# One chunk of RWKV-7 attention plus SwiGLU: the decayed neighbours of `a` laid out by distance first, and one ScalarE copy per level for both kept halves of K

## The chip, the cores and the metric

The kernel runs on one core of a Trainium2 chip. The metric is the device time of one execution in microseconds; the median of three runs is quoted. A core has five engines that each work through their own list in order: TensorE (PE, with weight loads shown as PEld), VectorE (DVE), ScalarE (ACT), GpSimd (POOL) and SyncE (SP). They wait for one another through semaphores. Transfers go through queues that SP, POOL and, at the start, ACT issue into.

## The reference

Two blocks, one after the other. The first is RWKV-7 attention over 4 batches, 8 heads, 768 steps and head size 40 (32 sequences in all), the second a SwiGLU feed-forward over the 3072 tokens of width 320 with hidden size 1536.

```python
for t in range(S):
    y[:, :, t] = np.einsum('bhd,bhde->bhe', rt, state)
    Sa = np.einsum('bhde,bhe->bhd', state, at)
    state_decay = state * wt[:, :, None, :] - np.einsum('bhd,bhe->bhde', Sa, bt)
    state = state_decay + np.einsum('bhd,bhe->bhde', vt, kt)
...
rms = np.sqrt(np.mean(x * x, axis=-1, keepdims=True) + 1e-06)
xn = x / rms * rms_g
g = xn @ w_gate
out = (g * (1.0 / (1.0 + np.exp(-g))) * (xn @ w_val)) @ w_out
```

## The kernel before, in words

**Chunks.** The 768 steps are cut into 24 chunks of C = 32. Inside a chunk the recurrence becomes a triangular system: how strongly step s reaches a later step t is the product of a vector of s (k or b), a vector of t (a), and all decays w between them. `front(c)` (line 654) loads a chunk, turns it on TensorE so that the 40 channels lie on partitions, and builds the triangular matrix LT and the decayed keys KN. `inverse(c)` (or `early_inverse` for the first four chunks) inverts the triangle on VectorE in small steps, with trips to DRAM and back. `main(c)` makes the outputs and the next state. `feed(g)` runs the feed-forward for every second chunk. `front` runs two chunks ahead of `main`.

**Levels.** LT is filled by five levels l = 1, 2, 4, 8, 16: at level l a segment of 2l steps is split in halves, and entries cross from the left half to the right one. K holds the keys of both kinds, k and b (the code's `x in range(2)`, the two "crossings"), 32 steps each; A holds `a`. After each level the left halves of K are multiplied by the decay of the right half, and the right halves are kept as they are; A likewise for the other side.

**Levels 1 and 2 in one step.** Inside a group of four steps there are six pairs: three at distance 1, two at distance 2, one at distance 3. The tile A holds, for each of 16 sequences on a partition block (NI) and each of 8 groups (g), seven vectors, some of them `a` itself and some `a` times decays. ScalarE copies three of them out of PSUM (line 681). VectorE makes entries 3 and 4 from entries 1 and 2 and the decays (line 690), and entry 6 from entry 4 (line 691). One set of small matmuls ("gramk", lines 693 and 694) multiplies K with all 56 columns of A into PSUM. Then three masked copies on VectorE (the helper `where`, a `copy_predicated`, lines 696 to 699) pick entries for distances 1, 2 and 3 out of PSUM into LT under the mask `near`. Lines 708 to 710 build from A the next level's tile Ab. The distances' first columns stand at 0, 3 and 6 of a group's seven.

**Levels 4, 8 and 16** (lines 713 to 750) each run gramk from Ab, one masked copy into LT under `msk`, a ScalarE copy of KN out of PSUM, a product of K's left halves on VectorE, and the copy of K's right halves into the other K tile on ScalarE (lines 730 and 731), once for each of the two crossings.

**Order.** Every operation is recorded as a piece; pieces wait for those that wrote or read the same elements. Nothing is scheduled at run time: the string ORDER lists, by place among the pieces not yet issued, which piece comes next, and a dash puts in a matmul that only keeps TensorE running (line 1017). PAIRS says which of three PSUM pairs each PSUM tile ("room") uses. Each engine's list follows from that order. Helpers record most operations, so profile lines are those of helpers: L446 is every VectorE operation, L469 a ScalarE copy, L488 a matmul, L491 a transpose.

Of the kernel before, what the change touches and what calls it, by code (L numbers as in the profile page):

```python
# [9 lines left out]
U32 = mybir.dt.uint32  # L10
# [7 lines left out]
P = 128  # L18
# [15 lines left out]
85 84 76 83 58 78 73 86 74 59 60 75 5 89 61 88 53 77 80 4 43 6 201 7 87 90 44 8 334 62 9 - - - - - - - - 93 10 18 79  # L34
11 12 214 557 13 213 567 14 15 94 566 210 16 17 95 558 108 200 - - - 97 96 19 335 20 21 2 209 22 23 98 25 199 568 26
100 578 202 24 101 107 569 111 57 - - - - - 102 106 124 589 27 122 112 392 109 103 52 119 113 104 54 577 155 125 110
204 105 120 - - - - - - 114 203 117 121 559 211 598 118 46 131 129 132 45 562 560 212 597 563 588 561 394 123 115 136
586 384 133 134 - - - - - 126 130 116 47 564 3 145 383 135 336 128 137 48 144 143 141 587 219 142 51 570 127 565 146
138 337 55 573 1005 216 579 281 393 220 582 608 571 390 234 379 239 607 572 583 580 380 251 574 222 38 221 609 575 581
42 - - - - - - - - 223 82 226 339 91 64 227 338 39 81 139 224 263 576 238 153 56 249 247 590 206 584 228 382 237 591  # L40
272 593 40 233 232 585 381 154 148 594 33 140 205 229 592 389 235 250 28 248 - - 325 236 32 245 36 230 147 260 282 391
246 259 150 35 34 326 595 0 36 270 155 214 148 242 243 62 605 598 230 - 239 40 616 599 601 628 64 49 91 600 602 30 48
626 1135 28 257 603 29 241 68 150 255 65 0 1347 194 0 194 84 173 0 - - - 182 540 200 0 557 184 1 186 935 542 540 0 506
515 527 257 513 300 0 111 97 110 61 112 96 51 439 458 122 50 243 480 0 244 0 58 255 242 0 259 709 104 120 246 708 247
456 470 258 488 719 0 256 470 457 242 0 716 265 487 104 0 268 0 0 265 473 0 262 277 0 273 0 236 0 260 0 269 0 461 241
- - - - - - - 237 242 0 0 278 242 243 252 0 252 0 0 89 0 99 246 0 97 0 230 94 440 0 230 94 440 231 - - - - - - - - -
240 441 244 0 0 468 440 451 255 0 42 468 269 469 258 215 440 239 204 0 0 257 253 203 93 449 92 212 0 235 - - - - - - -
- 246 0 437 0 262 0 246 247 436 245 464 470 258 259 469 260 244 - - 255 471 465 468 466 0 215 466 269 256 445 697 255
478 686 93 94 264 95 687 270 96 266 97 0 97 470 695 2 98 99 3 100 471 101 473 1 102 0 468 99 470 100 471 101 441 102
103 258 104 105 260 106 - - - - - - - - - - - 0 504 106 107 473 108 0 108 502 0 108 109 469 110 111 0 0 0 0 0 - - 13 0  # L50
374 16 146 143 14 147 142 15 13 355 - - - 25 386 358 0 358 386 388 16 387 389 25 390 79 17 391 28 70 147 355 191 69
356 80 148 149 26 359 0 28 2 29 149 0 149 150 29 0 149 31 185 391 23 32 390 29 150 356 151 186 33 389 0 151 29 387 152
27 40 187 153 154 155 156 33 157 158 159 160 161 34 162 36 163 164 37 165 41 391 38 42 392 39 394 561 166 395 393 552
0 42 548 395 209 0 560 165 42 395 548 210 43 428 211 427 557 44 - - - 565 166 558 45 167 549 168 0 566 168 739 565 567
738 571 169 579 - - 45 728 572 0 124 139 0 535 682 0 535 545 140 578 536 141 0 547 545 546 543 578 0 558 554 567 0 519
- - - - - - 517 377 696 378 380 381 695 518 120 685 135 526 - - - - - - 522 686 379 527 382 136 530 383 554 529 121 -
- 141 540 123 523 565 539 122 537 142 125 538 124 524 - - - - 145 525 148 534 149 152 154 551 535 147 555 - - 157 146
# [3 lines left out]
607 367 478 34 568 - - 35 830 594 36 567 820 38 - 476 37 571 366 570 0 605 356 433 434 435 436 120 437 0 317 318 319  # L61
320 441 321 322 323 324 355 456 458 459 442 4 357 325 457 326 327 328 443 0 443 328 329 330 331 357 0 35 331 3 0 37
450 359 3 36 358 331 332 357 333 356 0 462 448 330 461 464 331 332 468 364 447 463 31 467 476 458 333 365 334 335 0
425 439 441 302 426 436 0 6 439 2 0 435 332 2 436 443 444 0 448 332 442 334 443 333 340 449 0 297 329 342 32 330 - 3
33 341 334 0 332 331 0 332 293 441 295 333 0 438 0 436 333 336 295 337 309 438 338 1 375 342 310 365 374 515 27 292 0
362 292 26 28 44 339 29 34 27 32 338 0 646 29 34 336 647 32 0 439 64 315 647 339 440 634 441 63 340 0 287 413 606 312
313 607 623 12 314 615 414 0 410 310 411 603 619 27 412 475 413 620 414 415 621 416 311 633 28 417 812 418 312 625 - -
- - 476 313 419 420 421 822 258 314 422 423 0 810 423 625 637 477 2 0 819 2 257 0 420 421 645 310 422 0 - - - - - 310
422 3 313 32 630 311 423 33 643 424 641 631 312 0 0 637 20 635 420 647 613 21 421 611 648 819 23 38 22 422 809 423 39
659 24 3 612 36 818 424 651 25 808 621 425 59 660 426 249 427 58 0 427 3 25 428 249 4 28 47 0 - 614 428 429 28 430 431  # L70
0 26 25 614 617 484 31 27 627 0 458 590 400 600 401 0 12 582 32 401 33 583 25 0 579 30 21 - - - - - - - - - 588 29 591
22 453 397 428 398 605 23 0 23 429 24 609 0 590 24 397 588 602 1 604 398 601 429 430 399 2 427 0 584 - - - - - - - - -
- - - - - 4 397 0 25 397 4 0 393 394 28 21 23 27 395 598 24 22 424 607 0 35 395 37 396 24 2 424 47 397 398 38 399 400
# [4 lines left out]
976 716 416 663 729 634 977 562 563 717 713 986 665 564 565 566 975 567 401 568 714 569 985 570 571 967 572 723 722 -  # L78
0 403 726 402 572 401 573 0 726 738 736 573 739 574 664 575 737 576 577 3 723 751 578 579 760 580 747 581 582 633 583
4 584 0 584 585 634 586 636 587 635 588 734 633 0 746 588 - - - - - 403 757 589 722 590 3 404 591 592 593 594 595 596  # L80
# [290 lines left out]
def kernel(  # L371
# [42 lines left out]
    NI = 2 * N  # L414
# [239 lines left out]
    def front(c):  # L654
# [19 lines left out]
        o = 0  # L674
# [375 lines left out]
```

## Time and profile before

| what | us |
|---|---|
| three runs | 1083.66, 1079.48, 1078.9 |
| median | 1079.48 |
| span of the profiled execution | 1078.2 |
| TensorE busy | 1010.2 |
| VectorE busy | 834.2 |
| ScalarE busy | 462.2 |
| GpSimd busy | 309.0 |

The profiled execution is a run of its own, and its own time is known from its span alone: first to last instruction, without what lies before and after. A busy engine is one that has an instruction in work; on TensorE matmuls overlap, so being busy is not being at its peak. The stretch views give the busy time of each engine in a piece of the span. The group rows give how often an instruction with a shape ran, its total and its mean in ns, and then the idle time ahead of it with what ended that.

### The profile page before, as it was taken

To read this page: it belongs to the slowest core of one execution; us is meant where nothing else is said; L and a number is where in the kernel's file an instruction comes from. 1 tells how busy PE (TensorE), PEld (TensorE's weight loads), DVE (VectorE), ACT (ScalarE), POOL (GpSimd) and SP (SyncE) were. 2 spreads that over 40 slices of the span, in tenths; PEclk is the share of its full clock that TensorE was granted. 3 is DMA by queue.
4 is the path that set the end of the run, shared out by engine and by line. 5 is a ranking of instruction groups with operands and counts; after the bars stand their busy time and mean duration, and the time that the engine had idled before them with its cause. 6 is when DMAs were issued, how large, how long until landed. Compare 5 with 4: busy or idle time off the path is not lost. (4 is left out here: it accounts for less than half of the span.)

```text
span 1078.2 us, 53465 instructions
## 1 busy us (share of the span) xinstructions
PE 1010.2 (94%) x23406; PEld 828.3 (77%) x23406; DVE 834.2 (77%) x2861; ACT 462.2 (43%) x1043; POOL 309.0 (29%) x554
## 2 busy tenths in 40 slices
PE   6767899999999999999999999998999999999998
PEld 6766778777888787877788778887777887887776
DVE  7887879876868888887897888887788889797420
ACT  6845756643543433532443434433344344342211
POOL 9714404120532223241331331331332331200000
PEclk9778999999999999999999999999999999999999
DMA  9965448766564364574465654665545553744242
GB/s 180 196 155 123 73 106 220 213 127 177 124 142 122 99 150 116 144 145 120 96 152 133 146 126 112 142 142 123 126 106 110 134 150 90 162 109 123 77 140 86
DMA packets 172456, 143.34 MB, mean 133 GB/s; under 512 B 125504, under 2 KB 143872, under 8 KB 172224
## 3 DMA queue, kind: packets, MB, share of 16 engines
q1 hardware_dynamic: 153856, 116.96, 42.4%
q0 software_dynamic: 16192, 22.64, 12.2%
q8 instruction: 184, 3.01, 1.2%
q10 hardware_dynamic: 2176, 0.33, 0.2%
q14 instruction: 48, 0.39, 0.1%
HBM read 123.86 MB, written 15.99 MB: 130 GB/s over the span
## 5 line engine op out<-in xcount | busy, mean ns | idle before, releaser
L488 PE MATMUL ps<-xg,wf 128*128 128x256 f32 (+1 forms) x1728 | 355.2, 392 | 4.7 <-DVE xg L446 1.1
L488 PEld LDWEIGHTS ps<-xg,wf 128*128 128x128 f32 (+1 forms) x1728 | 261.6, 189 | 60.4 <-issue 16.9
L488 PE MATMUL po<-wf,hT 128*128 128x320 f32 x576 | 180.1, 445 | 0.1
L446 DVE TENSOR_TENSOR tmp<-Yi,M 128x60 f32<-128x60 f32 (+24 forms) x620 | 129.5, 209 | 19.7 <-DMA M<-sB 6.9
L446 DVE TENSOR_TENSOR Yi<-Yi,tmp 128x60 f32<-128x60 f32 (+24 forms) x620 | 130.2, 210 | 12.7 <-DVE ss L446 0.2
L466 ACT ACTIVATE sg<-ps 128x256 f32<-128x256 f32 x144 | 52.4, 383 | 192.4 <-PE ps L488 182.7
L488 PEld LDWEIGHTS po<-wf,hT 128*128 128x128 f32 x576 | 102.6, 191 | 34.0 <-issue 1.7
L485 POOL DMA_DIRECT2D VU<-in_v_dram x92 | 53.6, 587 | 234.2 <-PE ps L488 157.0
L446 DVE TENSOR_TENSOR hT<-ps,sg 128x256 f32<-128x256 f32 x144 | 59.0, 419 | 62.4 <-ACT sg L466 55.9
L469 ACT COPY KN<-ps 128x640 f32<-128x640 f32 x96 | 66.2, 691 | 76.6 <-PE ps L491 27.9
L488 PEld LDWEIGHTS ps<-Ab,K 40*64 40x64 f32 x4608 | 78.3, 139 | 26.4 <-issue 8.5
L446 DVE TENSOR_TENSOR K<-K,T 128x512 f32<-128x512 f32 (+1 forms) x192 | 93.3, 495 | 4.2 <-ACT K L469 2.1
L488 PE MATMUL ps<-Ab,K 40*64 40x56 f32 x4608 | 88.0, 225 | 8.8 <-ACT K L469 3.7
L485 POOL DMA_DIRECT2D kbn<-in_b_dram x92 | 53.4, 584 | 147.9 <-PE ps L488 147.0
L446 DVE TENSOR_TENSOR As<-ps,msi 128x256 f32<-128x256 f32 (+1 forms) x186 | 79.2, 475 | 18.3 <-PE ps L488 17.4
L469 ACT COPY K<-K 128x256 f32<-128x256 f32 (+1 forms) x168 | 71.8, 443 | 41.3 <-PE ps L488 20.3
L488 PEld LDWEIGHTS ps<-As,KN 128*40 128x40 f32 x3072 | 64.6, 122 | 15.1 <-issue 9.7
L485 POOL DMA_DIRECT2D wn<-in_w_dram x92 | 51.6, 565 | 83.7 <-DVE KN L446 34.7
L485 POOL DMA_DIRECT2D kbn<-in_k_dram x92 | 53.5, 585 | 73.8 <-PE ps L488 73.5
L488 PE MATMUL ps<-As,KN 128*40 128x32 f32 x3072 | 71.1, 203 | 3.7 <-issue 2.7
L446 DVE TENSOR_TENSOR y<-y,ps 128x256 f32<-128x256 f32 x119 | 49.9, 419 | 19.7 <-PE ps L488 17.6
L446 DVE COPY_PREDICATED LT<-near,ps 128x384 f32<-128x384 uint32 (+2 forms) x72 | 52.3, 727 | 3.6 <-PE ps L488 1.9
(133 smaller groups left out, 1544.5 us busy)
## 6 DMA issues: line engine op xcount, KB each, us to landing
wf<-sW SPq DMA_DIRECT2D x144, 480.0 KB, 4.3
M<-sB SPq DMA_DIRECT2D x80, 128.0 KB, 3.8
rn<-in_r_dram SPq DMA_DIRECT2D x24, 160.0 KB, 4.5
sW<-ex SPq DMA_DIRECT2D x16, 240.0 KB, 4.3
out_dram<-o SPq DMA_DIRECT2D x48, 80.0 KB, 3.9
kbn<-in_k_dram POOLq DMA_DIRECT2D x92, 40.0 KB, 3.5
kbn<-in_b_dram POOLq DMA_DIRECT2D x92, 40.0 KB, 3.3
wan<-in_a_dram POOLq DMA_DIRECT2D x46, 80.0 KB, 4.7
```

The costliest lines, as they stand in the source:

```text
L446: plan.add("DVE", kind, lambda at: fn(at(o), *m(at)), [o], aps(*args))
L466: plan.add("ACT", "act", lambda at: nc.scalar.activation(at(o), at(a), f, **kw), [o] + aps(acc), [a])
L469: plan.add("ACT", "copy", lambda at: nc.scalar.copy(at(o), at(a)), [o], [a])
L485: plan.add(by, "dma", lambda at: queue.dma_start(out=o, in_=i), [o], [i])
L488: return o, lhsT, rhs, lambda at: nc.tensor.matmul(at(o), lhsT, rhs, start=start, stop=stop, skip_group_check=True)
```

## The change

A is laid out as NI x 7 x 8 in place of NI x 8 x 7: for a sequence the eight groups of one entry now lie side by side, where before the seven entries of one group did. All that touch A follow: the copy out of PSUM, the products, gramk's right operand (still 56 floats in a row), the PSUM result (g4) and the masked copies, which now go entry by entry and within an entry over the eight groups. LT, `near`, the decays T and the tile Ab keep their layout; they are walked in the new order. Apart from that the two copies of K's right halves at levels 4, 8 and 16 become one over both crossings. ORDER names the pieces of the same order with the dropped copies left out, so its numbers differ; in each pair the single copy stands either where the first or where the second stood.

```diff
-    A_ = Turns(1, [P, NI, 8, 7], "A", whole)
+    A_ = Turns(1, [P, NI, 7, 8], "A", whole)
...
-        copy(A[:, :, :, 0:3], a4.rearrange("p n (g j) -> p n g j", j=4)[:, :, :, 1:4])
+        copy(A[:, :, 0:3], a4.rearrange("p n (g j) -> p n j g", j=4)[:, :, 1:4])
...
-        w4 = Tl[1].rearrange("p n (g j) -> p n g j", j=4)
         t2 = Tl[2].rearrange("p n (g x) -> p n g x", x=2)
-        tt(A[:, :, :, 3:5], A[:, :, :, 1:3], w4[:, :, :, 1:3], MUL)
-        tt(A[:, :, :, 6], A[:, :, :, 4], w4[:, :, :, 1], MUL)
+        w_j = Tl[1].rearrange("p n (g j) -> p n j g", j=4)
+        tt(A[:, :, 3:5], A[:, :, 1:3], w_j[:, :, 1:3], MUL)
+        tt(A[:, :, 6], A[:, :, 4], w_j[:, :, 1], MUL)
         gr = plan.room().rearrange("p o (n t) -> p o n t", n=N)
         pe("gramk", [mm(gr[half(i), o, n, 0:56], K[part(o), 2 * n + i].rearrange("p x s -> p (x s)"),
-                        A[part(o), 2 * n + i].rearrange("p g j -> p (g j)")) for n, i, o in each])
-        g4 = gr.rearrange("p o n t -> p (o n) t")[:, :, 0:56].rearrange("p n (g j) -> p n g j", j=7)
+                        A[part(o), 2 * n + i].rearrange("p j g -> p (j g)")) for n, i, o in each])
+        g4 = gr.rearrange("p o n t -> p (o n) t")[:, :, 0:56].rearrange("p n (j g) -> p n j g", g=8)
         for dist, at in ((1, 0), (2, 3), (3, 6)):
             m = 4 - dist
-            where(LT.rearrange("p n (g j) -> p n g j", j=4)[:, :, :, dist:], near[:, dist - 1:dist].rearrange(
-                "p u (g j) -> p u g j", j=4)[:, :, :, dist:].bitcast(U32).to_broadcast((P, NI, 8, m)), g4[:, :, :, at:at + m])
+            where(LT.rearrange("p n (g j) -> p n j g", j=4)[:, :, dist:], near[:, dist - 1:dist].rearrange(
+                "p u (g j) -> p u j g", j=4)[:, :, dist:].bitcast(U32).to_broadcast((P, NI, m, 8)), g4[:, :, at:at + m])
...
         for x in range(2):
-            tt(Ab[:, :, 16 * x:16 * x + 16].rearrange("p n (h j) -> p n h j", j=4)[:, :, :, 1:4], A[:, :, x::2, 0::3],
-               w4[:, :, x::2, 0:1].to_broadcast((P, NI, 4, 3)), MUL)
+            tt(Ab[:, :, 16 * x:16 * x + 16].rearrange("p n (h j) -> p n j h", j=4)[:, :, 1:4], A[:, :, 0::3, x::2],
+               w_j[:, :, 0:1, x::2].to_broadcast((P, NI, 3, 4)), MUL)
...
-            for x in range(2):
-                copy(side(K1[:, :, x], l, 1), side(K[:, :, x], l, 1))
+            both = lambda t_: side(t_.rearrange("p n x s -> p (n x) s"), l, 1)
+            copy(both(K1), both(K))
```

More of the change, by code (lines that the diff above doesn't have):

```diff
@@ L39 @@
[L39 to L53, printed above, removed]
@@ L62 @@
[L62 to L66, printed above, removed]
@@ L72 @@
-22 453 397 428 398 605 23 0 23 429 24 609 0 590 24 397 588 602 1 604 398 601 429 430 399 2 427 0 584 - - - - - - - - -
-- - - - - 4 397 0 25 397 4 0 393 394 28 21 23 27 395 598 24 22 424 607 0 35 395 37 396 24 2 424 47 397 398 38 399 400
[4 rows of a table removed]
-976 716 416 663 729 634 977 562 563 717 713 986 665 564 565 566 975 567 401 568 714 569 985 570 571 967 572 723 722 -
-0 403 726 402 572 401 573 0 726 738 736 573 739 574 664 575 737 576 577 3 723 751 578 579 760 580 747 581 582 633 583
-4 584 0 584 585 634 586 636 587 635 588 734 633 0 746 588 - - - - - 403 757 589 722 590 3 404 591 592 593 594 595 596
[147 rows of a table removed]
+85 84 76 83 58 78 73 86 74 59 60 75 5 89 61 88 53 77 80 4 43 6 198 7 87 90 44 8 328 62 9 - - - - - - - - 93 10 18 79
@@ new lines @@
+11 12 211 548 13 210 558 14 15 94 557 207 16 17 95 549 108 197 - - - 97 96 19 329 20 21 2 206 22 23 98 25 196 559 26
+100 569 199 24 101 107 560 111 57 - - - - - 102 106 123 580 27 121 112 386 109 103 52 113 104 54 568 152 124 110 119
+201 105 - - - - - - 114 200 117 120 550 208 589 118 46 130 128 45 553 551 209 588 554 579 552 388 122 115 134 577 378
+131 132 - - - - - 125 129 116 47 555 3 142 377 133 330 127 135 48 141 139 578 216 140 51 561 126 556 143 136 331 55
+564 993 213 570 275 387 217 573 599 562 384 231 373 236 598 563 574 571 374 247 565 219 38 218 600 566 572 42 - - - -
@@ new lines @@
+- - - - 220 82 223 333 91 64 224 332 39 81 137 221 258 567 235 150 56 245 243 581 203 575 225 376 234 582 266 584 40
+230 229 576 375 151 145 585 33 138 202 226 583 383 232 246 28 244 - - 319 233 32 242 36 227 144 255 276 385 254 147 35
+34 320 586 0 36 264 152 211 145 239 240 62 596 589 227 - 236 40 607 590 592 619 64 49 91 591 593 30 48 617 1120 28 594
+29 238 68 147 251 65 0 1329 189 0 189 81 170 0 - - - 178 531 194 0 548 180 1 182 923 533 531 0 497 506 518 251 504 294
+0 109 96 108 61 95 51 433 452 119 50 240 474 0 241 0 58 252 239 0 256 703 102 117 243 702 244 450 464 255 482 713 0
@@ new lines @@
+253 464 451 239 0 710 261 481 102 0 264 0 0 261 467 0 258 272 0 268 0 233 0 256 0 264 0 455 238 - - - - - - - 234 239
+0 0 272 239 240 249 0 0 0 87 0 96 243 0 94 0 227 91 434 0 227 91 434 228 - - - - - - - - - 237 435 241 0 0 462 434 445
+251 0 42 462 263 463 253 212 434 236 201 0 0 252 200 90 443 89 209 0 232 - - - - - - - - 242 0 431 0 256 0 242 243 430
+241 458 464 253 254 463 240 - - 250 465 459 462 460 0 212 460 263 251 439 691 250 472 680 90 91 258 92 681 264 93 260
+94 0 94 464 689 2 95 96 3 97 465 98 467 1 99 0 462 96 464 97 465 98 435 99 100 252 101 102 254 103 - - - - - - - - - -
@@ new lines @@
+- 0 498 103 104 467 105 0 105 496 0 105 106 463 107 108 0 0 0 0 0 - - 13 0 371 16 143 140 14 144 139 15 13 352 - - -
[3 rows of a table added]
+43 425 208 424 554 44 - - - 562 163 555 45 164 546 165 0 563 165 733 562 564 732 568 166 576 - - 45 722 569 0 121 136
+0 532 676 0 532 541 137 572 533 138 0 543 541 542 539 572 0 553 549 561 0 516 - - - - - - 514 374 690 375 377 378 689
+515 117 679 132 523 - - - - - - 519 680 376 524 379 133 527 380 549 526 118 - - 138 120 520 559 536 119 534 139 122
+535 121 521 - - - - 142 522 145 531 146 149 151 547 532 144 550 - - 154 143 546 533 147 152 148 551 162 558 150 157
@@ new lines @@
+685 161 158 686 0 158 683 159 162 1 0 542 670 0 503 41 551 42 553 43 419 504 986 552 44 987 45 560 506 420 430 434 433
+421 431 568 505 438 432 441 46 569 823 439 0 569 439 582 832 570 574 0 832 45 442 574 46 822 584 570 586 443 572 47
+594 48 597 11 840 585 571 440 608 593 830 0 11 440 370 595 0 580 590 601 367 475 34 565 - - 35 824 589 36 564 814 38 -
[3 rows of a table added]
+329 436 331 437 330 337 443 0 294 326 339 32 327 - 3 33 338 331 0 329 328 0 329 290 435 292 330 0 432 0 430 330 333
+292 334 306 432 335 1 372 339 307 362 371 509 27 289 0 359 289 26 28 44 336 29 34 27 32 335 0 640 29 34 333 641 32 0
@@ new lines @@
+433 64 312 641 336 434 628 435 63 337 0 284 407 600 309 310 601 617 12 311 609 408 0 404 307 405 597 613 27 406 469
+407 614 408 409 615 410 308 627 28 411 803 412 309 619 - - - - 470 310 413 414 415 813 255 311 416 417 0 801 417 619
+631 471 2 0 810 2 254 0 414 415 638 307 416 0 - - - - - 307 416 3 310 32 624 308 417 33 636 418 634 625 309 0 0 630 20
+628 414 639 607 21 415 605 640 810 23 38 22 416 800 417 39 650 24 3 606 36 809 418 643 25 799 615 419 59 651 420 246
+421 58 0 421 3 25 422 246 4 28 47 0 - 608 422 423 28 424 425 0 26 25 608 611 478 31 27 0 452 584 593 394 395 0 12 576
@@ L228 @@
+32 395 33 577 25 0 573 30 21 - - - - - - - - - 582 29 585 22 447 391 422 392 23 0 23 423 24 601 0 584 596 24 391 582
+595 1 392 594 423 424 393 2 421 0 578 - - - - - - - - - - - - - - 4 391 0 25 391 4 0 387 388 28 21 23 27 389 590 24 22
[5 rows of a table added]
+395 559 705 560 973 561 562 955 563 714 713 - 0 397 717 396 563 395 564 0 717 728 726 564 729 565 655 566 727 567 568
+3 714 740 569 570 748 571 736 572 573 624 574 4 575 0 575 576 625 577 627 578 626 579 724 624 0 735 579 - - - - - 397
[145 rows of a table added]
 """
```

15 lines of the change are left out of this document (removed), and 310 rows, old and new, of the table ORDER.

## The prediction

> **What bounds the kernel now.** I read the page first, for each engine's load; then stretches of 45 us, for where TensorE stands still; then the groups with shapes kept apart, for prices; last the chain of waits and the timeline, for what reaches the end.
>
> ```profile
> PE 1010.2 (94%) x23406; PEld 828.3 (77%) x23406; DVE 834.2 (77%) x2861; ACT 462.2 (43%) x1043; POOL 309.0 (29%) x554
> ```
> ```profile
> 0.00:45.00 45.00, 32.56 (x656) 29.71 (x657) 37.67 (x101) 33.23 (x67) 41.68 (x93) 0.90 0.95 176
> 45.00:90.00 45.00, 32.98 (x832) 29.88 (x831) 32.49 (x114) 26.32 (x50) 10.92 (x22) 0.76 0.68 164
> 450.00:495.00 45.00, 44.21 (x973) 35.89 (x972) 40.34 (x152) 18.66 (x44) 11.70 (x20) 1.00 0.63 142
> 855.00:900.00 45.00, 42.97 (x972) 35.15 (x971) 37.77 (x138) 18.30 (x44) 14.68 (x25) 1.00 0.52 123
> ```
>
> In the stretches the columns after the length are PE, PEld, DVE, ACT and POOL busy. TensorE is nearly full in the middle (44.2 and 43.0 of 45 us) and loses 12 us in each of the first two stretches, so little can be won later on. VectorE is second with 5 to 7 us of idle time in each middle stretch, ScalarE has half of its time free. What makes an engine other than TensorE faster can win only where TensorE waits for it; what makes VectorE slower costs whatever its idle time does not take up. Here is what it does around the instructions that change, from the chain of waits:
>
> ```profile
> 905.44 0.66 DVE LT L446
> 906.12 0.74 DVE LT L446
> 907.30 0.64 DVE LT L446
> ...
> 937.14 0.73 DVE LT L446
> 937.89 0.74 DVE LT L446
> 938.65 0.72 DVE LT L446
> 939.44 0.81 PE ps L488 x64
> ```
>
> These are the three masked copies into LT (the `where` loop, lines 696 to 699) of two late chunks. All six are links of the chain that ended last; after the second triple TensorE starts at once.
>
> **The change, part by part.** Orders first: on TensorE, VectorE, GpSimd and SyncE the program has the same instructions in the same order; ScalarE has 72 fewer. No transfer, queue or semaphore partner is added, and the moving operand of the matmuls stays 56 floats in a row. So the time goes by the durations of the instructions with new access patterns.
>
> ```profile
> L446 DVE COPY_PREDICATED LT<-near,ps 128x128 f32<-128x128 uint32 x24 | 17.5, 729 | 0.4
> L446 DVE COPY_PREDICATED LT<-near,ps 128x256 f32<-128x256 uint32 x24 | 17.4, 726 | 0.3
> L446 DVE COPY_PREDICATED LT<-near,ps 128x384 f32<-128x384 uint32 x24 | 17.4, 726 | 2.9 <-PE ps L488 1.9 <-DMA out_dram<-o 0.8
> L446 DVE COPY_PREDICATED LT<-msk,ps 128x256 f32<-128x256 uint32 x72 | 31.2, 433 | 13.8 <-PE ps L488 8.8 <-ACT KN L469 3.8
> L446 DVE TENSOR_TENSOR T<-T 128x128 f32<-128x128 f32 x24 | 6.8, 285 | 0.1
> L446 DVE TENSOR_TENSOR T<-T 128x256 f32<-128x256 f32 x24 | 10.1, 420 | 4.0 <-ACT T L469 3.9
> ```
>
> *Masked copies.* The striking thing is that 128, 256 and 384 elements take the same 726 to 729 ns, while the later levels' masked copies do 256 in 433. In the first three, 128 groups (16 sequences by 8) are walked, with 3, 2 or 1 elements each: the price is per group. The two T rows give an ordinary slope of (420 - 285) / 128 = 1.05 ns an element; then 433 - 256 x 1.05 = 164 ns is a masked copy's fixed part, and a group costs (729 - 164) / 128 = 4.4 ns, however many of its four neighbours are taken. Why per group? Three operands step there: LT and `near` by 4 floats from group to group, PSUM by 7. The cost is the same for one element as for three, though three cover more of PSUM; what all three share is one 4-float place in LT and one in `near` per group. I put the price there.
>
> After the change the inner loop runs over the 8 groups for one distance, then over the next. That is exactly the walk that the 729 ns instruction does already (LT and `near` by 4 floats, one element at each stop; only PSUM goes from steps of 7 to steps of 1). So 384 elements become three such walks: 164 + 3 x 565 = 1859 ns, 256 two: 1294, 128 one: 729. Sum 3.88 us instead of 2.18: **+1.70 us a chunk**. The other end: if the PSUM step alone is the price, it goes, and at 1.05 ns an element they take 567, 433 and 298 ns, -0.88 us. I take +1.70, since the 729 ns row is the nearest there is.
>
> [...]
>
> *The products.*
>
> ```profile
> L446 DVE TENSOR_TENSOR A<-A,T 128x256 f32<-128x256 f32 x24 | 11.0, 460 | 3.5 <-ACT T L469 3.5
> L446 DVE TENSOR_TENSOR A<-A,T 128x128 f32<-128x128 f32 x24 | 9.6, 398 | 0.2
> L446 DVE TENSOR_TENSOR Ab<-A,T 128x192 f32<-128x192 f32 x48 | 20.9, 441 | 0.2
> ```
>
> The second walks lone elements (A by 7, w by 4) and takes 398 against 285 for 128 closer elements: with a fixed part of 285 - 128 x 1.05 = 150 ns that is 1.94 ns an element. Afterwards A lies in a row but w (in T) is still read by 4 or 8, and Ab is written by 4. Bounds: 420 to 150 + 256 x 1.94 = 647 for the first, 285 to 398 for the second, 352 to 522 for each of two Ab. Against 460 + 398 + 2 x 441 that is -0.35 to +0.35 us a chunk; I take +0.35, as a lone step remains in each. VectorE in all: +2.05 us a chunk, 49 us over 24.
>
> *ScalarE.*
>
> ```profile
> L469 ACT COPY K<-K 128x256 f32<-128x256 f32 x144 | 55.7, 405 | 40.9 <-PE ps L488 20.3 <-DVE K L446 14.5 <-issue 4.8
> L469 ACT COPY K<-K 128x512 f32<-128x512 f32 x24 | 16.2, 673 | 0.4
> L469 ACT COPY A<-ps 128x384 f32<-128x384 f32 x24 | 13.9, 581 | 3.4 <-PE ps L491 3.4
> L469 ACT COPY Ab<-ps 128x128 f32<-128x128 f32 x24 | 9.6, 398 | 4.2 <-PE ps L491 4.2
> L469 ACT COPY M<-ps 128x128 f32<-128x128 f32 x8 | 2.2, 272 | 5.5 <-PE ps L488 4.3 <-DMA wf<-in_moe_w_out_dram 1.2
> L469 ACT COPY T<-ps 128x512 f32<-128x512 f32 x24 | 14.2, 591 | 15.2 <-PE ps L491 10.9 <-DVE tmp L446 2.9 <-DVE Yi L446 1.3
> L469 ACT COPY K<-ps 128x1024 f32<-128x1024 f32 x24 | 24.3, 1011 | 19.0 <-PE ps L491 19.0
> ```
> ```profile
> PEld ps L488 <- ACT K L469: 11.0, 12, 3.8
> PE ps L488 <- ACT K L469: 7.2, 5, 3.7
> ```
> ```profile
> 739.64 0.71 ACT L469 COPY K<-K 128x256 f32<-128x256 f32 x2
> ```
>
> Two copies of 256 become one of 512: 2 x 405 to at most 673 (that row steps by 2; this one has runs of 4, 8 or 16). Neighbouring copies overlap, a pair is through in 0.71 us (last row), so a pair wins some 0.04 to 0.1 us. The single copy must wait for both crossings' halves of K, where the first of two waited for one; behind it stands most often the KN copy, for whose PSUM room a later gram waits. In the program's order 28 of the 72 pairs stand together; of the other 44 the single copy stands at the first one's place in 18, at the second's in 25, in between once. At the first's place it is ready sooner and delays what stood between (mostly KN copies) by 0.27 us; at the second's it ends up to 0.27 us later. TensorE waits for these copies 18.2 us in 17 waits. 17 x 0.27 = 4.6 us either way is the bound; I take 0.
>
> A's copy out of PSUM now reads by 4 floats. Bounds: from 591 - 128 x 0.83 = 484 ns (slope (1011 - 591) / 512) up to that plus 384 x (398 - 272) / 128 = 862. I take +0.28 us, by the Ab row, and cost it at nothing: ScalarE next stands 19.0 us in all, 0.8 a chunk, waiting for TensorE before K's copy. Without that cover it costs 24 x 0.28 = 6.7 us.
>
> *What reaches the end.* VectorE is in order, so all behind the masked copies moves: the K products, the next level's masked copy, the inverse's steps, hT. Who waits: the gram matmuls of the next level, hence KN and K on ScalarE. In the two chunks of the chain all 2.05 us count. For the two before them I read the slack from the timeline, between the last masked copy and the gram matmuls that follow:
>
> ```profile
> 823.61 0.73 DVE L446 COPY_PREDICATED LT<-near,ps 128x128 f32<-128x128 uint32 x1
> ...
> 860.48 0.72 DVE L446 COPY_PREDICATED LT<-near,ps 128x128 f32<-128x128 uint32 x1
> ```
> ```profile
> 825.48 1.16 PE L488 MATMUL ps<-Ab,K 40*64 40x56 f32 x64
> ...
> 862.03 1.16 PE L488 MATMUL ps<-Ab,K 40*64 40x56 f32 x64
> ```
>
> That is 825.48 - 824.34 = 1.14 and 862.03 - 861.20 = 0.83 us, which leaves 0.91 and 1.22 late. The mean of four is 1.56 us a chunk, 37 us for 24. TensorE's idle 1 to 2 us of each 45 us takes up part of a lateness from chunk to chunk; I estimate a fifth, which leaves **+30 us**. The span is 1078.2 us, 1.3 below the median of 1079.5 (runs 1078.9 to 1083.7); I add to the median: 1109.5, say **1109 us**. Ends of this case: half of the 24 delays count in full and the others not at all, less the product term, 12 x 1.35 = +16 (1095), to all 49 us (1128).
>
> **Rivals.**
>
> *PSUM's step of 7 was the price* (the faster side). Place: the same three copies. It decides if the 729 ns fall to about 298 when only the PSUM step changes. For it: PSUM is what differs most from the 433 ns row (there 16 floats in a row). Against: equal time for one, two and three PSUM elements. Price: -0.88 + 0.35 = -0.53 us a chunk, down to -1.2 with the low products; where the copies are on the chain (2 of 4) that is 12 x 0.53 = -6 to 12 x 1.2 = -15: 1065 to 1073, say 1072. [...]
>
> *A lone stop costs a masked copy what it costs a product*, 1.94 ns an element, and the rest was PSUM. Then 164 + 1.94 x (384, 256, 128) = 909, 661, 412, sum 1.98: -0.20, with the products +0.15 us. By 1.56 / 2.05 of that, 24 x 0.11 = +3 us: 1082. For it: the 398 ns row has the same steps in SBUF. Against: it needs PSUM to make up just the difference in all three.
>
> **How the numbers follow.** Forecast 0.72, PSUM rival 0.17, middle rival 0.11. About 0.5% (5.4 us) is what a measurement of this kernel can tell from no change, so same is 1074 to 1085. The forecast falls whole on slower, the PSUM rival on faster (0.16, with 0.01 too small to tell), the middle one mostly on same (0.09; 0.02 slower with ScalarE's +4.6). Faster 0.16, same 0.10, slower 0.74. The range 1077 to 1127 takes the forecast and the middle rival and leaves out the PSUM rival and the top.
>
> **What would show it.** Masked copies of 1.86, 1.29 and 0.73 us: the forecast's price. 0.57, 0.43, 0.30: the PSUM rival. 0.91, 0.66, 0.41: the middle. The 128-element copy alone decides, since only its PSUM step changes. Products near 640, 400 and 520 ns; A's copy near 860; K copies near 620 to 670 and 72. VectorE near 883 us busy; TensorE's busy time about as now, so its idle time up by the 30 us. Wrong I would be if VectorE gets the 49 us and TensorE's idle time does not grow: then its slack is larger than in the four chunks read.

## The result and the profile after

The changed kernel takes **1121.35 us** (median of 6 runs, 1111.99 to 1128.05) where the kernel before takes 1079.19 us (6 runs): a ratio of 1.0361, 95% interval 1.0313 to 1.0408. It is slower by 42 us; 30 us were forecast, inside a range that ended at 1127. A ratio leaves out any execution more than 1.5% above the fastest of its kernel, so it can differ a little from the quotient of two medians. The profiled execution of the changed kernel took 1125.09 us, with a span of 1122.8 us. After the change the helpers' lines lie three lower: L443 is every VectorE operation, L466 a ScalarE copy, L485 a matmul, L488 a transpose, L1014 the warm matmuls.

The page's first line for the changed kernel, and TensorE's rows of the 40 slices:

```profile
PE 1033.0 (92%) x23406; PEld 847.4 (75%) x23406; DVE 883.0 (79%) x2861; ACT 453.5 (40%) x971; POOL 309.7 (28%) x554
...
PE   6778899999999998999999999998998999999998
...
PEclk8786889999999999999999999999989999999999
```

The same two rows of the kernel before:

```profile
PE   6767899999999999999999999998999999999998
...
PEclk9778999999999999999999999999999999999999
```

VectorE is busy 883.0 us, 48.8 more than before. TensorE's idle time rose from 1078.2 - 1010.2 = 68.0 to 1122.8 - 1033.0 = 89.8 us, and its busy time rose as well, by 22.8 us for the same 23406 matmuls. So in this pair of profiles half of the longer span is waiting and half is matmuls that take longer. Of the six executions this one has the lowest granted clock, 0.954 (the others 0.956 to 0.974). In two later profiled executions of the same kernel (e8 and e11 below) TensorE's idle time is the same, 89.6 and 90.2 us, but its busy time is 1024.6 and 1022.2 us, 14 and 12 us more than before and not 23. PEclk has 8, 6, 8 and 8 in the third to sixth slice where it had 7, 8, 9 and 9. By stretches (after the length PE, PEld, DVE, ACT and POOL busy, then the granted clock, DMA's share and GB/s), those that the prediction showed of before and the third one:

```profile
45.00:90.00 45.00, 33.50 (x668) 30.21 (x668) 36.37 (x118) 26.46 (x51) 12.06 (x25) 0.69 0.67 163
90.00:135.00 45.00, 39.85 (x1247) 36.22 (x1239) 36.54 (x102) 25.08 (x52) 17.91 (x33) 0.75 0.41 88
...
450.00:495.00 45.00, 42.62 (x1152) 34.99 (x1150) 37.71 (x129) 14.89 (x35) 16.87 (x29) 1.00 0.54 129
...
855.00:900.00 45.00, 41.70 (x943) 33.60 (x937) 37.96 (x121) 15.28 (x36) 11.06 (x19) 0.96 0.46 111
```

The third stretch of the kernel before:

```profile
90.00:135.00 45.00, 37.10 (x1278) 32.79 (x1271) 37.04 (x110) 28.02 (x67) 21.30 (x39) 0.96 0.47 95
```

From 90 to 135 us the changed kernel's TensorE is *busier* (39.85 for 37.10) with *fewer* matmuls (1247 for 1278): the clock there is 0.75 for 0.96. A busier engine at a lower clock is no better used. In the middle and late stretches it stands still for 2.4 and 3.3 us, where it was 0.8 and 2.0.

The groups with shapes kept apart, changed kernel:

```profile
L443 DVE COPY_PREDICATED LT<-near,ps 128x384 f32<-128x384 uint32 x24 | 44.8, 1865 | 2.7 <-PE ps L485 1.9 <-DMA out_dram<-o 0.7
L443 DVE COPY_PREDICATED LT<-near,ps 128x256 f32<-128x256 uint32 x24 | 31.0, 1291 | 0.3
L443 DVE COPY_PREDICATED LT<-near,ps 128x128 f32<-128x128 uint32 x24 | 17.4, 725 | 0.4
...
L443 DVE TENSOR_TENSOR A<-A,T 128x256 f32<-128x256 f32 x24 | 15.1, 630 | 3.2 <-ACT T L466 1.6 <-ACT A L466 1.5
L443 DVE TENSOR_TENSOR A<-A,T 128x128 f32<-128x128 f32 x24 | 9.3, 388 | 0.2
L443 DVE TENSOR_TENSOR Ab<-A,T 128x192 f32<-128x192 f32 x48 | 24.4, 515 | 0.2
...
L466 ACT COPY A<-ps 128x384 f32<-128x384 f32 x24 | 12.1, 503 | 2.4 <-PE ps L488 2.4
L466 ACT COPY K<-K 128x512 f32<-128x512 f32 x96 | 60.7, 632 | 44.7 <-DVE K L443 29.4 <-PE ps L485 12.7 <-DVE Yi L443 1.9
```

The three masked copies now take 1865, 1291 and 725 ns. That is (1865 + 1291 + 725) - (726 + 726 + 729) = 1700 ns more a chunk, 40.8 us in 24 chunks. The products take (630 + 388 + 2 x 515) - (460 + 398 + 2 x 441) = 308 ns more, 7.4 us. Together that is 48.2 of the 48.8 us. And where TensorE waits for them, in the list of waits (us in all, times, the longest):

```profile
PE ps L485 <- DVE K L443: 12.4, 7, 3.8
PEld ps L485 <- DVE LT L443: 10.5, 8, 2.6
PE ps L485 <- DVE LT L443: 9.4, 8, 2.1
...
PE ps L485 <- ACT K L466: 0.6, 1, 0.6
```

In the kernel before the same waits came to this:

```profile
PEld ps L488 <- DVE LT L446: 2.8, 6, 0.9
...
PE ps L488 <- DVE K L446: 1.8, 2, 0.9
...
PE ps L488 <- DVE LT L446: 0.4, 1, 0.4
```

TensorE's matmuls waited 0.4 us for LT and now wait 9.4 in 8 times. Their waits for K grew less than the first row says: before, 7.2 us more were waits for ScalarE's copies of K (the row stands in the prediction), so it is 9.0 us before and 13.0 after. Another wait behind the masked copies is in the last chunk, in the timeline (start, us, what; in brackets the idle time ahead of it):

```profile
978.67 3.92 DVE L443 COPY_PREDICATED LT<-near,ps 128x384 f32<-128x384 uint32 x3
978.96 1.34 PE L485 MATMUL po<-wf,hT 128*128 128x320 f32 x4
...
982.65 1.29 PE L485 MATMUL ps<-Xs,LT 32*32 32x40 f32 x64 [2.34 <-DVE tmp L443]
```

Before, the last of the three copies ended at 938.65 + 0.72 = 939.37 and TensorE's next matmuls started at 939.44. Now TensorE is done at 980.30 and stands 2.34 us, until the copies end at 982.59. (The bracket names `tmp`, VectorE's next instruction, which ends 0.05 us after the copies. In the semaphore's records the copies' end is 0.04 us ahead of this start and that of `tmp` 0.01 us behind it, and it is the same in the kernel before; so the copies are what ends the wait.)

### The profile page after: what moved, and what is told of

Same layout as the page of the kernel before. It is cut to its first block, busy times and chain, and to the rows that moved or that the text cites. A ratio compares the mean times of both kernels' runs of the same rounds, so it can differ in the third digit from the quotient of the medians.

```text
span 1122.8 us, 53387 instructions
## 1 busy us (share of the span) xinstructions
PE 1033.0 (92%) x23406; PEld 847.4 (75%) x23406; DVE 883.0 (79%) x2861; ACT 453.5 (40%) x971; POOL 309.7 (28%) x554
## 5 line engine op out<-in xcount | busy, mean ns | idle before, releaser
L485 PE MATMUL ps<-xg,wf 128*128 128x256 f32 (+1 forms) x1728 | 362.1, 397 | 8.9 <-DVE hT L443 2.3
L485 PEld LDWEIGHTS ps<-xg,wf 128*128 128x128 f32 (+1 forms) x1728 | 265.8, 192 | 66.5 <-issue 15.6
L485 PE MATMUL po<-wf,hT 128*128 128x320 f32 x576 | 179.1, 443 | 0.8 <-DVE hT L443 0.7
L443 DVE TENSOR_TENSOR tmp<-Yi,M 128x60 f32<-128x60 f32 (+24 forms) x620 | 130.7, 211 | 19.2 <-DMA M<-sB 6.3
L443 DVE TENSOR_TENSOR Yi<-Yi,tmp 128x60 f32<-128x60 f32 (+24 forms) x620 | 131.2, 212 | 12.3
L485 PEld LDWEIGHTS po<-wf,hT 128*128 128x128 f32 x576 | 102.0, 190 | 34.7 <-DVE hT L443 1.7
L485 PE MATMUL ps<-Ab,K 40*64 40x56 f32 x4608 | 91.4, 232 | 29.6 <-DVE K L443 12.0
L485 PEld LDWEIGHTS ps<-Ab,K 40*64 40x64 f32 x4608 | 81.7, 145 | 48.1 <-issue 18.7
L443 DVE TENSOR_TENSOR hT<-ps,sg 128x256 f32<-128x256 f32 x144 | 59.4, 422 | 61.3 <-ACT sg L463 54.5
L466 ACT COPY KN<-ps 128x640 f32<-128x640 f32 x96 | 66.2, 691 | 92.3 <-DVE LT L443 33.4
L443 DVE TENSOR_TENSOR K<-K,T 128x512 f32<-128x512 f32 (+1 forms) x192 | 94.8, 503 | 6.2 <-PE ps L485 3.3
L443 DVE COPY_PREDICATED LT<-near,ps 128x384 f32<-128x384 uint32 (+2 forms) x72 | 93.2, 1294 | 3.3 <-PE ps L485 1.9
L443 DVE TENSOR_TENSOR As<-ps,msi 128x256 f32<-128x256 f32 (+1 forms) x186 | 79.4, 476 | 15.7 <-PE ps L485 14.2
L466 ACT COPY K<-K 128x512 f32<-128x512 f32 x96 | 60.7, 632 | 44.7 <-DVE K L443 29.4
L485 PEld LDWEIGHTS ps<-As,KN 128*40 128x40 f32 x3072 | 66.4, 125 | 13.4 <-issue 8.2
L485 PE MATMUL ps<-As,KN 128*40 128x32 f32 x3072 | 72.5, 206 | 2.2 <-issue 1.2
L443 DVE TENSOR_TENSOR y<-y,ps 128x256 f32<-128x256 f32 x119 | 49.9, 419 | 20.8 <-PE ps L485 18.7
```

Source lines behind the costliest of these rows:

```text
L443: plan.add("DVE", kind, lambda at: fn(at(o), *m(at)), [o], aps(*args))
L466: plan.add("ACT", "copy", lambda at: nc.scalar.copy(at(o), at(a)), [o], [a])
L485: return o, lhsT, rhs, lambda at: nc.tensor.matmul(at(o), lhsT, rhs, start=start, stop=stop, skip_group_check=True)
```

## The experiments

Theory at the start: a masked copy pays about 4.4 ns for each lone place it touches, the new walk turns places that held two or three elements into lone ones, and the lateness reaches the end through VectorE's order. Rivals: another part of the change carries the loss (the layout's products, the single K copy), or the price is in PSUM or in the mask. Later, once the trace showed TensorE's busy time up: the waits also cost granted clock. The experiments ran in four sets; each ratio is against the kernel before, run on the same chip in the same set (medians 1073.5 us for e1 to e4, 1074.1 for e5 to e8, 1077.5 for e9 to e11, 1074.6 for e12).

**e1, the layout and its walks, with two K copies.**

```diff
-            both = lambda t_: side(t_.rearrange("p n x s -> p (n x) s"), l, 1)
-            copy(both(K1), both(K))
+            for x in range(2):
+                copy(side(K1[:, :, x], l, 1), side(K[:, :, x], l, 1))
```

> A by distance and the new walks as in the changed kernel, but K's kept halves copied in two steps as before, in the order of before. Theory (the masked copies and products are all of it, the single copy of K is worth nothing): masked copies 1865, 1291 and 725 ns, VectorE near 883 us busy, time 1115 to 1125 us. Rival (the single copy, put in 25 of 72 pairs at the second one's place, is what took the time beyond the +30 forecast): 1106 to 1112 us.

Measured: 1119.58 us, ratio 1.0413 (1.0356 to 1.047), masked copies of 1868, 1291 and 725 ns. The whole loss is there without the single K copy, and the time lies in the theory's range, not in the rival's.

**e2, the single K copy alone, in the old layout** (the reverse of e1's diff, made to the kernel before).

> A, its products and the masked copies as before; only the single copy of K per level, in the changed kernel's order. Theory: no difference, 1076 to 1082 us, ScalarE some 9 us less busy. Rival (the single copy ends later where it stands at the second one's place): 25 x 0.27 = 7 to 12 us more, 1086 to 1091 us.

Measured: 1075.25 us, ratio 1.0017 (0.9989 to 1.0045), K copies of 618 to 620 ns at levels 4, 8 and 16. What the single copy wins or costs can't be told from nothing; by the interval it is at most 4.8 us.

**e3, only the order in which the masked copies walk**, in the old layout, so that PSUM is still read by 7.

```diff
-            where(LT.rearrange("p n (g j) -> p n g j", j=4)[:, :, :, dist:], ...
-                "p u (g j) -> p u g j", ...), g4[:, :, :, at:at + m])
+            where(LT.rearrange("p n (g j) -> p n j g", j=4)[:, :, dist:], ...
+                "p u (g j) -> p u j g", ...), g4[:, :, :, at:at + m].rearrange("p n g j -> p n j g"))
```

> Everything as before, the masked copies alone walk by distance first (LT and near by 4 floats from element to element, PSUM by 7). Theory (a lone stop in LT and near costs 4.4 ns wherever PSUM goes): 1860, 1290 and 727 ns, VectorE 41 us busier than before, time 1079 + 42 x 41 / 49 = 1110 to 1118 us. Rival (dense PSUM rows or the new products carry part of the loss): under 1100 us or other durations of the masked copies.

Measured: 1112.29 us, ratio 1.0368 (1.0323 to 1.0413). Its three groups:

```profile
L446 DVE COPY_PREDICATED LT<-near,ps 128x384 f32<-128x384 uint32 x24 | 44.8, 1865 | 3.9 <-PE ps L488 3.7
L446 DVE COPY_PREDICATED LT<-near,ps 128x256 f32<-128x256 uint32 x24 | 30.9, 1290 | 0.3
L446 DVE COPY_PREDICATED LT<-near,ps 128x128 f32<-128x128 uint32 x24 | 17.4, 724 | 0.4
```

The same three durations as in the changed kernel, with PSUM by 7 instead of by 1, and nearly the whole loss. The walk is the price, and PSUM's step has no part in it.

**e4, the new layout with the old walk** (group by group, PSUM by 8 from element to element): e3's edit reversed, made to the changed kernel.

> A by distance and the single copy of K as in the changed kernel, but the masked copies walk group by group again (LT and near 3, 2 or 1 floats in a row, PSUM by 8 within the row). Theory (price per place in LT and near, not per element and not by PSUM): all three near 726 ns, the new products remain, 0.31 x 24 = +7 us of VectorE, time 1080 to 1087 us. Rival (lone PSUM elements, 8 apart, are what a masked copy pays for): the 384-element copy near 1.8 us and most of the loss stays, over 1105 us.

Measured: 1078.42 us, ratio 1.005 (1.0022 to 1.0078).

```profile
L443 DVE COPY_PREDICATED LT<-near,ps 128x128 f32<-128x128 uint32 x24 | 17.5, 730 | 0.4
...
L443 DVE COPY_PREDICATED LT<-near,ps 128x384 f32<-128x384 uint32 x24 | 17.4, 724 | 3.1 <-PE ps L485 2.2 <-DMA wf<-sW 0.7
```

With the old walk all three are back at 724 to 730 ns. What is left, 4.9 us of time for 7.5 us more of VectorE (841.7 busy), goes with the products: e2 found nothing in the single K copy, and the copy of A out of PSUM got shorter. e3 and e4 together give 38.8 + 4.9 = 43.7 us, the change's loss (42 to 44 us in the result, e8 and e11).

**e5, the mask in a row**: `near` is stored by distance, so that the copies read it without gaps; LT is still written by 4.

```diff
-        ts(near[:, dist], bits, float(dist + 1), None, ALU.is_equal)
-        tt(near[:, dist], near[:, dist], same, MUL)
+        nd = near[:, dist].rearrange("p (j g) -> p g j", g=8)
+        by_g = lambda t: t.rearrange("p (g j) -> p g j", j=4)
+        ts(nd, by_g(bits), float(dist + 1), None, ALU.is_equal)
+        tt(nd, nd, by_g(same), MUL)
...
-                "p u (g j) -> p u j g", j=4)[:, :, dist:].bitcast(U32) ...
+                "p u (j g) -> p u j g", g=8)[:, :, dist:].bitcast(U32) ...
```

> The changed kernel, but the mask near is stored by distance first, so the masked copies read it in a row; LT is still written 4 floats apart, PSUM is read in a row. Which operand sets the 4.4 ns of a lone place is open. If the written one (LT) alone does: 1865, 1291, 725 ns as before. If both add: about 1.0, 0.7, 0.43 us. If the mask alone does: about 0.57, 0.43, 0.30 us.

**e6, the target in a row**: LT is written without gaps, `near` is still read by 4.

```diff
-            where(LT.rearrange("p n (g j) -> p n j g", j=4)[:, :, dist:], ...
+            where(LT.rearrange("p n (j g) -> p n j g", g=8)[:, :, dist:], ...
```

> The changed kernel, but the masked copies write LT in a row, so levels 1 and 2 land in the wrong places of LT and the output is not the reference's; the mask is still read 4 floats apart. If the written operand alone sets the price: about 0.57, 0.43, 0.30 us. If both add: about 1.0, 0.7, 0.43 us. If the mask alone does: 1865, 1291, 725 ns. VectorE 25 to 50 us less busy than the changed kernel in the first two cases and a time of 1075 to 1095 us.

Measured, in a single run of each: e5 1114.44 us, e6 1079.03 us. The widest copy of e5, then the three of e6:

```profile
L443 DVE COPY_PREDICATED LT<-near,ps 128x384 f32<-128x384 uint32 x24 | 44.7, 1862 | 2.7 <-PE ps L485 1.8 <-DMA out_dram<-o 0.7
```
```profile
L443 DVE COPY_PREDICATED LT<-near,ps 128x384 f32<-128x384 uint32 x24 | 20.2, 843 | 3.1 <-PE ps L485 2.2 <-DMA out_dram<-o 0.7
L443 DVE COPY_PREDICATED LT<-near,ps 128x256 f32<-128x256 uint32 x24 | 14.7, 611 | 0.3
L443 DVE COPY_PREDICATED LT<-near,ps 128x128 f32<-128x128 uint32 x24 | 9.2, 385 | 0.3
```

The mask in a row changes nothing (1862 ns). The target in a row takes 4.4 ns an element down to (843 - 385) / 256 = 1.79. So the lone places *written* set the price. The 843, 611 and 385 ns of e6 lie between two of the cases that were named for it. What is left is not the 1.05 ns of copies in a row: the likeliest reason is the mask, still read by 4, but the two together in a row were not tried.

**e7, more warm matmuls**, to see what the clock is worth: 140 more dashes at 35 places of ORDER where TensorE stood still for over 0.6 us in the changed kernel (each dash is two matmul records); one place as an example. **e8** is the changed kernel again, beside it.

```diff
-... 240 - - 250 465 459 ...
+... 240 - - - - - - - - - - - - 250 465 459 ...
```

> The changed kernel with 140 more of the matmuls that only keep TensorE running, put at 35 places where the changed kernel's trace has TensorE idle for over 0.6 us, filling some 60% of each gap. Theory (the +42 us are about +30 of waits and +12 of a lower granted clock after these waits): the mean granted clock rises from 0.96 to 0.975 or more, and the time falls by 6 to 12 us against the changed kernel on the same chip. Rival (the waits alone cost the 42, the clock only shows that TensorE waits): the clock rises and the time stays within 3 us or grows by what the matmuls take.

> The changed kernel once more, on the chip of the other three, so that they have a partner: ratio to the kernel before 1.031 to 1.042 as measured, masked copies 1865, 1291, 725 ns, VectorE 883 us.

Measured: e7 1127.24 us, ratio 1.0499 (1.0446 to 1.0552), granted clock 0.978 to 0.984; e8 1117.51 us, ratio 1.0442 (1.0369 to 1.0515), clock 0.956 to 0.963. In e7 the clock is back at the old kernel's, TensorE's matmuls other than the warm ones fall from 974.3 to 962.0 us and its idle time from 89.6 to 79.0, but the warm ones grow by 34.3 us. The theory had the time fall by 6 to 12 us; it is 10 us longer than e8's, so on the time the rival was right. As a remedy that is a loss; whether the clock costs time it could not tell. (e8's own ratio lies a little above the range named for it.)

**e9, distance 3 by a product**, made to the kernel before: the copy that writes one lone element a group becomes a `tensor_tensor` of PSUM and mask, first of the three.

```diff
-        for dist, at in ((1, 0), (2, 3), (3, 6)):
+        for dist, at in ((3, 6), (1, 0), (2, 3)):
...
+            if dist == 3:
+                tt(o_n, g4[:, :, :, at:at + m], m_n.to_broadcast((P, NI, 8, m)), MUL)
+            else:
+                where(o_n, m_n.bitcast(U32).to_broadcast((P, NI, 8, m)), g4[:, :, :, at:at + m])
```

> The kernel before, with distance 3 first and as a plain product of PSUM with the mask (it writes 0 where the mask is 0, and distances 1 and 2 then write over it as masked copies). If a lone place in the written operand costs 4.4 ns only under a masked copy and 1.9 ns under a product: 729 becomes about 400 ns, VectorE 8 us less busy, and at the share of VectorE's time that reached the end so far (0.65 to 1) 3 to 8 us less, 0.3 to 0.7%. If a lone place costs 4.4 ns whatever the operation: no difference in the instruction or the time.

Measured: 1075.17 us, ratio 0.9974 (0.9938 to 1.001), VectorE 6.8 us less busy.

```profile
L446 DVE TENSOR_TENSOR LT<-ps,near 128x128 f32<-128x128 f32 x24 | 9.2, 384 | 2.9 <-PE ps L488 1.9 <-DMA out_dram<-o 0.8
```

The same 128 places, steps and operands take 384 ns in a product and 729 ns in a masked copy. The time can't be told from no change. How much of the 6.8 us reaches the end stays open: the interval goes from 6.7 us less to 1.1 us more.

**e10, warm matmuls early only**: 63 dashes at 14 places ahead of 235 us, where most of the low clock lies. **e11** is the changed kernel beside it.

> The changed kernel with 63 more of the matmuls that only keep TensorE running, at 14 places before 235 us alone, where 75 of its 105 us at half clock lie and where TensorE is idle for 10 us of each 45. If the low clock after the waits lengthens the run there: granted clock 0.97 or more, other matmuls 7 to 10 us less busy, time 3 to 8 us less than the changed kernel's. If the clock costs nothing beside the waits: the same time within 3 us or more.

> The changed kernel as a partner of the one with early extra matmuls on the same chip: ratio to the kernel before 1.036 to 1.044.

Measured: e10 1111.77 us, ratio 1.0328 (1.0269 to 1.0387), clock 0.970 to 0.987; e11 1121.62 us, ratio 1.0403 (1.0341 to 1.0465), clock 0.959 to 0.965. The page's first lines, e10 and then e11:

```profile
PE 1026.1 (93%) x23532; PEld 841.6 (76%) x23532; DVE 881.0 (79%) x2861; ACT 453.2 (41%) x971; POOL 312.1 (28%) x554
```
```profile
PE 1022.2 (92%) x23406; PEld 838.2 (75%) x23406; DVE 880.5 (79%) x2861; ACT 453.4 (41%) x971; POOL 311.7 (28%) x554
```

The warm matmuls of the two:

```profile
L1029 PE MATMUL po<-ident 128*128 128x128 f32 x428 | 62.3, 299 | 3.3 <-DVE po L531 3.3
```
```profile
L1014 PE MATMUL po<-ident 128*128 128x128 f32 x302 | 50.7, 323 | 4.7 <-DVE po L516 3.3 <-issue 1.4
```

With 126 matmul records more, e10 is 10 us quicker by the medians. Its other matmuls take 1026.1 - 62.3 = 963.8 us for e11's 971.5, its idle time is 83.0 for 90.2. The two intervals overlap a little, and the two profiled executions differ by 3.3 us in span alone (1109.1 and 1112.4: 11.6 us more of warm matmuls, 7.7 less of others, 7.2 less of idle time). So the 10 us are a size of the effect and not its measure; that the clock was lifted by early work is plain.

**e12, both together on the kernel before**: e9's edit and 44 dashes at ten early places.

> The kernel before with the distance-3 entries made by a product instead of a masked copy (384 ns for 729 in the run where this alone was tried) and 44 more warm matmuls at ten places before 235 us where TensorE stood still for over 0.6 us. Theory (waits early in the run cost granted clock, and the clock costs time): the clock rises from the .966 to .980 of the kernels in the old layout to .985 or more, TensorE's other matmuls get shorter by 3 to 6 us, VectorE stays near 827 us busy, and the time is 1068 to 1074 us beside a kernel before of 1074 to 1079, ratio 0.990 to 0.997. Rival (with few early waits the clock has little to give back, and 44 matmuls at 0.2 to 0.3 us cost what they win): ratio 0.997 to 1.003, warm matmuls near 58 us busy for 47.

Measured: 1110.44 us, ratio 1.0339 (1.0302 to 1.0375), clock 0.966 to 0.978. Both cases named were wrong by some 35 us. TensorE's waits for nothing that the profile shows, in the kernel before, in e9 and then in e12:

```profile
PE ps L488 <- issue: 21.9, 29, 1.9
```
```profile
PE ps L488 <- issue: 17.0, 24, 1.7
```
```profile
PE ps L502 <- issue: 43.0, 36, 3.9
```

One of them in e12's timeline:

```profile
602.62 0.28 PE L502 MATMUL ps<-r,Sd 40*40 40x32 f32 x2 [2.69 <-issue]
```

From e9 to e12 these waits grew by 26 us, from the kernel before by 21. The spans of e12 and e9 differ by 22.6 us (1104.3 and 1081.7; e9's profiled execution took 1083.89 us, 8.7 above its median): TensorE's idle time is 75.3 us for 59.7, its warm matmuls 58.7 for 50.4. The trace gives them a pattern. One DMA queue carries transfers of the kind `instruction`; its row in e12:

```profile
q8 instruction: 185, 3.03, 1.1%
```

That is 185 blocks of 16.4 KB. If they carry TensorE's list, which no record says, 3.03 MB over 2 x 23494 loads and matmuls is 64.5 bytes each, and a block would hold some 127 pairs, an estimate. In e12, 25 of the 43 stalls over 0.5 us (30.4 us in all) end 1.15 to 1.5 us after such a block has landed; in e9 it is 12 of 37 (13.1 us). By chance a stall would end so in about one case in 17 (185 x 0.35 us of 1104). Five stalls in a row start at matmuls 3903, 4156, 4538, 4666 and 4794, a multiple of about 127 apart. So TensorE most likely stood waiting for its program. That the 88 early records moved the borders of all later blocks onto stretches of small matmuls, which by that estimate would use up a block soonest, fits this, but no run moved the borders alone. The kernels e1 to e6 have the same list of matmuls as the kernel before, and in the changed kernel only 12 stalls (13.2 us) are of this kind, in the kernel before 16 (16.2 us): by these counts the change's own loss has no part of it. In e7 it is 18 (20.4 us).

## Why the prediction was right or wrong

**Masked copies: right, with its reason.** 1859, 1294 and 729 ns were worked out, 1865, 1291 and 725 measured. The prediction put the price on the places in LT and `near` and not on PSUM. e3 bears out that PSUM has no part; e5 and e6 split the rest: it is LT, the operand written. By the rows of before, a place with one element cost 4.4 ns, three neighbours in one place (726 - 164) / 384 = 1.46 ns each. That it was the write that paid most, four times the 1.05 ns of elements close together, e5 (1862 ns) and e6 (843 ns) show. PSUM's step decided nothing here: 724 to 730 ns with PSUM by 7 (the kernel before) and by 8 (e4), 1865 with PSUM by 7 (e3) and by 1 (the changed kernel).

**Products: right.** Forecast 647, 398 and 522 ns; measured 630, 388 and 515. (The low end of the range of -0.35 to +0.35 us a chunk comes to -0.33 by its own rows.) VectorE was to reach "near 883 us busy", and has 883.0.

**ScalarE's copy of A: wrong, without effect.** 862 ns was taken, 503 measured, close to the low bound of 484 and below the 581 of before. So reading PSUM by 4 costs ScalarE at most some 20 ns here; the old 581 came most likely from writing groups of three with a gap, which no run tried alone. The Ab row that the estimate leaned on reads by 8 and writes by 4, and its price was laid on the reading.

**K copies: right.** 618 to 620 ns, at the low end of the 620 to 673 forecast, and worth 0 as far as e2 can tell.

**What reaches the end: too small.** "TensorE's idle 1 to 2 us of each 45 us takes up part of a lateness from chunk to chunk; I estimate a fifth, which leaves +30 us." VectorE got 48.8 us more to do, and the time grew by 42 (0.86 of it, not 0.61); in e3 by 39 for 40.4. The lateness can be followed at the same three copies of the sixth chunk and of the last one, in the answers for the tile LT (durations least, median and most; first and last start), before:

```profile
L446 DVE COPY_PREDICATED LT<-near,ps x3: 726/729/744, 187.5 to 189.0; 128x384 f32<-128x384 uint32 x1, 128x256 f32<-128x256 uint32 x1, 128x128 f32<-128x128 uint32 x1
...
L446 DVE COPY_PREDICATED LT<-near,ps x3: 718/725/727, 937.1 to 938.7; 128x384 f32<-128x384 uint32 x1, 128x256 f32<-128x256 uint32 x1, 128x128 f32<-128x128 uint32 x1
```

and after:

```profile
L443 DVE COPY_PREDICATED LT<-near,ps x3: 722/1294/1889, 199.5 to 202.8; 128x384 f32<-128x384 uint32 x1, 128x256 f32<-128x256 uint32 x1, 128x128 f32<-128x128 uint32 x1
...
L443 DVE COPY_PREDICATED LT<-near,ps x3: 723/1278/1851, 978.7 to 981.9; 128x384 f32<-128x384 uint32 x1, 128x256 f32<-128x256 uint32 x1, 128x128 f32<-128x128 uint32 x1
```

The first start is 199.5 - 187.5 = 12.0 us late in the sixth chunk and 978.7 - 937.1 = 41.6 in the last: 29.6 / 18 = 1.64 us a chunk between. In e8 and e11, the same kernel, these starts come at 198.3 and 191.5 us in the sixth chunk and at 969.8 and 969.4 in the last: 10.8 and 4.0 us late, then 32.7 and 32.3, which is 1.22 and 1.57 us a chunk between. So the traces bear out the size of the slack (1.56 us late a chunk, 1.25 after the fifth is taken off), and they can't tell whether the fifth was too much. The first five chunks, in the stretches whose clock is lowest, lost 4 to 12 us where 5 x 1.25 = 6.2 had been reckoned.

**"TensorE's busy time about as now, so its idle time up by the 30 us": the step that failed.** The sum had no term for a longer busy time and gave no reason for leaving it out. Idle time rose by 21.8 us, busy time by 22.8, and in e8 and e11 idle by 22 and busy by 14 and 12. Of the busy time the warm matmuls, by their rows of before and after, are

```profile
L1017 PE MATMUL po<-ident 128*128 128x128 f32 x302 | 47.3, 307 | 6.3 <-DVE po L519 3.3 <-issue 3.0
```
```profile
L1014 PE MATMUL po<-ident 128*128 128x128 f32 x302 | 51.6, 328 | 3.3 <-DVE po L516 3.3
```

4.3 us; all others went from 962.9 to 981.4. The mean granted clock fell from 0.980 to 0.954; by the records of the clock TensorE ran at half speed for 45 us before and for 105 us after, three quarters of it ahead of 235 us. The busy time goes with that clock: in the eleven profiles with the same 23406 matmuls it rises by some 9 us for each 0.01 of clock lost, from 1009.2 us at 0.978 (e6) over 1014.7 at 0.974 (e4), 1018.7 at 0.972 (e1) and 1024.6 at 0.963 (e8) to 1033.0 at 0.954, and at 0.966 it is 1022.0 us with the old walk (e9) and 1022.8 with the new one (e5). So part of a wait was most likely paid twice, once standing and once at the lower clock that followed. In e10, with the clock at 0.980, the loss is 34 us, near the 30 forecast. How many of the 42 us are the clock's is known roughly. In e8 and e11 the mean clock is 0.961, and 0.976 in the kernel before beside them; at 9 us for each 0.01 that makes some 14 us, an estimate. e10 says about 10, with intervals that overlap; among the six runs of the changed kernel a clock higher by 0.01 goes with 6 us less, but what slows a run can also lower its clock. That 42 us fell inside the range is in part luck: its upper end let nearly all of VectorE's 49 us through, and the clock had no place in it.

**The rivals.** PSUM's step as the price and lone stops at a product's 1.94 ns both asked for a copy of 128 elements below 420 ns; it has 725.

## What to carry to other kernels

In a strided copy, look first at how many separate places are written and keep the inner loop on neighbours there (384 elements took 726 ns in 128 places and 1865 in 384); for one lone element a group, where zeros may be written beside the mask, a product with the mask took half the time of a masked copy (384 ns in e9 for 729). An engine that is "not the bound" but stands in a chain with the bound may hand on nearly all that is added to it (42 of 48.8 us here), so read the slack in several chunks. When TensorE waits more, look at its granted clock too (0.980 before, 0.954 after), and leave room for longer matmuls in the sum (22.8 us here). A few matmuls put into a gap can lift the clock (0.970 to 0.987 in e10 for 0.959 to 0.965 in e11), but the same means, with e9's edit, made another kernel 35 us slower (e12): measure each.

## What the runs showed of the hardware that was not expected

- The masked copies into LT on VectorE paid 4.4 ns for each place they wrote to ((1865 - 725) / 256 = 4.45 in the changed kernel), 4 floats from the last, whether one element was written there (729 ns for 128 places before) or three (726 ns); with the target in a row they took 1.79 ns an element (e6). A product with the same places took (384 - 150) / 128 = 1.83 ns (e9), with the fixed part of 150 ns that the prediction worked out.
- ScalarE's copy out of PSUM by 4 into a row took 503 ns for 384 elements in the changed kernel, little more than the estimate for a read in a row (484).
- TensorE's clock fell to half in pieces that are multiples of 3.4 us, each right behind a window of 3.4 us in which TensorE was busy for a share of 0.23 to 0.71 (worked out from the records of the kernel before and the changed one, without the last piece of each), in most of them about half; the longest single stall ahead of them was mostly 1.4 to 2.3 us. Other windows as empty were followed by the full clock (0.49 from 49.3 us on and 0.51 from 69.8 us on in the kernel before), so the share alone does not decide.
- TensorE seems to have stood still for its own program: stalls over 0.5 us that end 1.15 to 1.5 us after an `instruction` block of 16.4 KB has landed come to 16.2 us in the kernel before, 13.2 in the changed one and 30.4 in e12. That they are waits for the program is inferred from this pattern.
